# A ring of four places for the first raw weights, sums of four rows on VectorE for the second batch, and an earlier rank for it

## The chip, the cores and the metric

The kernel runs on one core of a Trainium2 chip. The metric is the time of one execution on the device in microseconds (us). A profile holds one execution; its time is the span of the trace and a little around it.

## What is computed

There are 8 batches, 8 heads, 576 positions and 64 columns in a head. The attention has two parts that are added: a global one on q, k and v averaged over groups of four rows, its result repeated four times, and a local one in which a row sees the rows less than four away. Heads side by side give x, 576 rows of 512 columns. Then x is mixed along the sequence and goes through a feed-forward network (FFN):

```python
q_d = q.reshape(B, H, S // 4, 4, D).mean(axis=3)          # k_d, v_d alike
x   = repeat(softmax(q_d k_d^T / 8) v_d, 4) + softmax(local q k^T / 8) v
u   = x + transpose(transpose(x) @ U @ V)                  # U 576 x 32, V 32 x 576
out = u + relu(u @ w_ch1) @ w_ch2                          # 512 -> 2048 -> 512
```

The weights, U and V come as 8-byte floats.

## The kernel before, in words

**Order of the work.** Every piece is an `op` with an engine, a duration, a rank (`prio`; lower goes first) and the buffers that it reads and writes. The class `Plan` is a list scheduler: it takes the ready op of the lowest rank on each engine, hands buffers out in the order in which they were asked for, and so writes a fixed order for each of the five engines TensorE (PE), VectorE (DVE), ScalarE (ACT), GpSimd (POOL) and SyncE (SP). All DMAs are issued from SP's one queue, which stands still where one of them has to wait.

**Batch 0.** Its four pairs of heads ("pair 0" to "pair 3") come first, each with `early_global` (scores `ps_s`, transposes `ps_t`, `ps_a`), `local_blocks` (`ps_b`, `ps_bt`, `ps_ba`) and `early_mix` (`ps_c`, `ps_x` into xT; `ps_hu`, which is x times U; then `ps_u`, which is added to xT on DVE at L743). From xT come uH on ACT and uL on POOL (L748).

**Weights.** There are 32 chunks of 511.8 KB, W1_0 to W1_15 and W2_0 to W2_15, read in the order W1_0 to W1_3, W1_4, W2_0, W1_5, W2_1 and so on up to W1_15 and W2_11 to W2_15. `load_w` asks for a raw buffer `wr`, issues its copy (L419), and `convert` makes the two halves of the chunk: ACT writes `half` (L347), DVE writes `y` (L350) and `c` (L352), ACT writes the high half W (L358), POOL the low half (L362). The raw buffer lies in the place in which the chunk itself will lie. `half` is one buffer, so conversions run in the order of the chunks. A copy waits until the conversion four chunks back has its `c`.

**FFN.** The tiles of columns are 4 of 288 (batches 0 and 1) and 9 of 384. A tile has 16 steps. `ffn1` of a step is 12 matmuls into `ps_h` (L959); ACT makes hH from it (L967), DVE hL (L968); `ffn2` is 12 matmuls into `acc` (L984), three steps later or more. Up to the nineteenth step, all but the second `ffn1` write the same PSUM bank, so that an `ffn1` waits for the hL before it.

**Batches 1 to 7.** Their attention lies between the FFN's steps: `late_global` (loads gq, gT and vr; sums of four rows; scores L790 and L783 in `ps_b`; `ps_t` L555; `ps_a` L569; stores up_s), `local_attn` (windows vl and ul, products Pt on POOL at L852, sums on DVE at L857, store x_s), `mix_part` (xL and Y from x_s; `ps_hu` L931; stk L936; `ps_u` L739). The sums of four rows are two POOL additions each: gh (L440) and smq or smk (L442) for q and k, and two (L530, L532) for each half of v. The buffers of these batches can be used only after the last op of batch 0's attention (`open_late`). `LEAD` is taken off the rank of batch 1's `late_global`. The first tile of batch 1 is tile 2: its FFN needs u of all four pairs.

## Time and profile before

| what | value |
|---|---|
| median of three runs | 1005.71 us (1005.45 to 1009.53) |
| the profiled execution | 1006.59 us |
| its span | 1004.8 us |
| PE busy in the span | 973.8 us, 97% |
| POOL, DVE, ACT busy | 571.8, 437.9, 345.4 us |
| mean granted clock of PE | 0.989 |

PE is busy nearly throughout, so that a time is read by where PE stood still or ran at half its clock, and by what it waited for there. The FFN begins at 66.46 us; the weights are all converted by about 122 us; tile 2 begins at 197.84 us.

### The profile page before, as it was taken

Reading aid. Unit: us, or ns where it says so; the run is one execution under the profiler, and the core shown is the slowest. Engines: PE = TensorE matmul, PEld = TensorE weight load, DVE = VectorE, ACT = ScalarE, POOL = GpSimd, SP = SyncE. Lnnn points to the kernel's source line nnn. Section 1 sums busy time; section 2 is a strip of 40 time slices with the busy share of each in tenths; the row PEclk is TensorE's granted clock in tenths of the full one; section 3 lists DMA queues with packets and bytes.
Section 4 is the critical chain, followed back from the end, with each engine's and each line's share of the span. In section 5 each row is a group of like instructions: output and inputs, shape, how many; then the busy total and the mean of one; then the engine's idle time right before and its main releaser. Section 6 shows DMA issues by size and latency. Waiting matters only on the chain.

```text
span 1004.8 us, 24588 instructions
## 1 busy us (share of the span) xinstructions
PE 973.8 (97%) x9896; PEld 940.5 (94%) x9896; DVE 437.9 (44%) x814; ACT 345.4 (34%) x1012; POOL 571.8 (57%) x640
## 2 busy tenths in 40 slices
PE   6879999899999999999999999999999999999998
PEld 4659999899999999999999999999999999999998
DVE  5686656535554444454434524354254222211211
ACT  4677544433343333243333233333332222111110
POOL 6586988957968657866665856665756112300100
PEclk9899999999999999999999999999999999999999
DMA  8949767647667546665454456465542021000000
GB/s 265 323 136 268 188 164 169 137 110 165 155 140 156 136 104 146 153 128 147 112 142 102 116 112 136 84 158 129 124 112 58 20 60 24 32 1 1 32 1 32
DMA packets 220906, 120.04 MB, mean 119 GB/s; under 512 B 174052, under 2 KB 196920, under 8 KB 220792
## 3 DMA queue, kind: packets, MB, share of 16 engines
q1 hardware_dynamic: 220792, 118.47, 48.0%
q8 instruction: 78, 1.28, 0.6%
q14 instruction: 36, 0.29, 0.1%
HBM read 87.57 MB, written 30.86 MB: 118 GB/s over the span
## 4 chain that ended last, share of the span: by engine, by line
PE 84%; DMA 4%; DVE 2%; SPq 1%; POOL 1%; issue 1%; ACT 0%; DVEq 0%; ACTq 0%
PE acc L984 37%; PE ps_h L959 37%; PE ps_a L569 2%; PE ps_b L790 2%; PE ps_t L555 2%; DMA wr<-in_W 2%; PE ps_hu L931 2%; PE ps_b L783 2%; DMA gq<-in_qT 1%; PE ps_u L739 1%; DVE acc L857 1%; DMA ul<-up_s 1%; DMA vr<-in_v 0%; POOL Pt L852 0%; SPq L806 0%
## 5 line engine op out<-in xcount | busy, mean ns | idle before, releaser
L984 PE MATMUL acc<-hH,W 128*128 128x384 f32 (+1 forms) x1664 | 443.1, 327 | 0.0
L959 PE MATMUL ps_h<-uH,W 128*128 128x384 f32 (+1 forms) x1376 | 358.1, 322 | 2.2 <-DVE hL L968 2.2
L984 PEld LDWEIGHTS acc<-hH,W 128*128 128x128 f32 x1664 | 297.6, 188 | 2.6
L984 PE MATMUL acc<-hL,W 128*128 128x384 f32 (+1 forms) x832 | 268.4, 323 | 0.0
L852 POOL TENSOR_TENSOR Pt<-vl,ms 128x896 f32<-128x896 f32 (+1 forms) x140 | 239.0, 1786 | 42.3 <-DMA vl<-in_vp 30.3
L968 DVE SCALAR_TENSOR_TENSOR hL<-ps_h,hH 128x384 fp32r<-128x384 f32 (+1 forms) x208 | 109.0, 524 | 331.0 <-ACT hH L967 330.5
L959 PEld LDWEIGHTS ps_h<-uH,W 128*128 128x128 f32 x1376 | 245.1, 189 | 3.5 <-DVE hL L968 2.6
L967 ACT ACTIVATE hH<-ps_h 128x384 fp32r<-128x384 f32 (+1 forms) x208 | 97.3, 468 | 370.2 <-PE ps_h L959 362.0
L959 PE MATMUL ps_h<-uL,W 128*128 128x384 f32 (+1 forms) x688 | 220.8, 321 | 1.6 <-POOL uL L748 1.6
L857 DVE TENSOR_REDUCE acc<-Pt 128x128 f32<-128x1024 f32 (+1 forms) x140 | 152.7, 1108 | 63.3 <-POOL Pt L852 29.7
L984 PEld LDWEIGHTS acc<-hL,W 128*128 128x128 f32 x832 | 156.8, 188 | 0.0
L959 PEld LDWEIGHTS ps_h<-uL,W 128*128 128x128 f32 x688 | 130.0, 189 | 1.8 <-POOL uL L748 1.8
L959 PE MATMUL ps_h<-u,W 128*128 128x384 f32 x432 | 98.1, 334 | 0.0
L846 ACT ACTIVATE Pt<-ul 128x128 f32<-128x128 f32 (+1 forms) x140 | 55.2, 436 | 91.3 <-DVE acc L857 62.3
L748 POOL TENSOR_TENSOR uL<-xT,uH 128x384 fp32r<-128x384 f32 (+2 forms) x52 | 40.9, 808 | 70.2 <-ACT uH L746 70.2
L923 POOL TENSOR_TENSOR xL<-xL,xH 116x640 fp32r<-116x640 f32 x28 | 43.8, 1566 | 61.9 <-ACT xH L922 50.7
L994 POOL TENSOR_TENSOR o<-uH,uL 128x384 f32<-128x384 f32 (+1 forms) x43 | 38.9, 936 | 70.0 <-DMA out_t<-o 70.0
L959 PEld LDWEIGHTS ps_h<-u,W 128*128 128x128 f32 x432 | 77.0, 188 | 0.0
L530 POOL TENSOR_TENSOR vr<-vr 72x256 f32<-72x256 f32 x56 | 41.1, 734 | 43.2 <-DMA vr<-in_v 41.5
L362 POOL TENSOR_TENSOR W<-c,W 128x512 fp32r<-128x512 f32 x32 | 40.8, 1283 | 18.1 <-ACT W L358 18.1
L743 DVE TENSOR_TENSOR xT<-ps_u,xT 128x384 f32<-128x384 f32 (+2 forms) x64 | 27.3, 451 | 28.1 <-PE ps_u L739 27.7
L790 PE MATMUL ps_b<-smk,smq 64*32 64x144 f32 x672 | 38.4, 292 | 0.0
(133 smaller groups left out, 893.3 us busy)
## 6 DMA issues: line engine op xcount, KB each, us to landing
wr<-in_W SPq DMA_DIRECT2D x32, 511.8 KB
vl<-in_vp SPq DMA_DIRECT2D x56, 240.0 KB
vr<-in_v SPq DMA_DIRECT2D x64, 144.0 KB
gT<-in_kT SPq DMA_DIRECT2D x28, 291.0 KB
gq<-in_qT SPq DMA_DIRECT2D x28, 288.0 KB
up_s<-od SPq DMA_DIRECT2D x168, 48.0 KB
ul<-up_s SPq DMA_DIRECT2D x28, 288.0 KB
x_s<-acc SPq DMA_DIRECT2D x28, 288.0 KB
```

The costliest lines, as they stand in the source:

```text
L362: pool_tt(1.0 * n, lambda: nc.gpsimd.tensor_tensor(out=lo_out(), in0=ta()[l0:], in1=hi_out()[l0:].bitcast(F32), op=ALU.subtract), [t, *own ...
L530: pool_tt(256, lambda x=x: nc.gpsimd.tensor_tensor(out=x()[:, :, 0:2, :], in0=x()[:, :, 0:2, :], in1=x()[:, :, 2:4, :], op=ALU.add), [x], ...
L748: pool_tt(n, lambda uH=uH, uL=uL, uf=uf, us=us: nc.gpsimd.tensor_tensor(out=uL.ap(hp, us), in0=uf(), in1=uH.ap(hp, us).bitcast(F32), op=AL ...
L790: nc.tensor.matmul(pg()[m:m + QL, a * SD:(a + 1) * SD], sq()[o, n:n + QL], sk()[o], start=True, stop=True)
L846: act(n * D, lambda n=n, ps=ps, Pt=Pt: nc.scalar.activation(Pt()[:, :n, :, 7], ul()[:, ps, :], AF.Copy), [ul], [(Pt, 1)], prio, 0.16)
L852: nc.gpsimd.tensor_tensor(out=Pt()[:, :n, :, 0:7].rearrange("p s d o -> p o s d"), in0=win, in1=at()[:, ps, :].rearrange("p s o -> p o s") ...
L857: dve(8.5 * n * D, lambda n=n, ps=ps, Pt=Pt: nc.vector.tensor_reduce(out=acc()[:, ps, :], in_=Pt()[:, :n], axis=AX.X, op=ALU.add), [(Pt, 0 ...
L923: pool_tt(640, lambda: nc.gpsimd.tensor_tensor(out=xL(), in0=xL().bitcast(F32), in1=xH().bitcast(F32), op=ALU.subtract), [xL, xH], [xL], prio)
L959: nc.tensor.matmul(ps()[:, :tn], W1[fc]()[:, w, dc, :], u.ap(dc), start=(n == 0), stop=(n == 3 * NDC - 1))
L967: last_h[i] = act(tn, lambda: nc.scalar.activation(hH()[:, :tn], ps()[:, :tn], AF.Relu), [ps], [hH], FIRST, 0.05)
L968: dve(tn, lambda: nc.vector.scalar_tensor_tensor(hL()[:, :tn], ps()[:, :tn], 0.0, hH()[:, :tn].bitcast(F32), op0=ALU.max, op1=ALU.subtract ...
L984: nc.tensor.matmul(ac[e]()[:, :tn], W2[fc]()[:, w, es], hx()[:, :tn], start=(fc == 0 and n == 0), stop=(fc == NFC - 1 and n == 2))
```

## The change

The first sixteen chunks no longer have their raw bytes in their own places: these go round a ring of four, the places of W2_11, W2_10, W1_15 and W1_14. (The first of them holds the table `pool` until `ps_p` has read it, the second pair 0's `vr`.) `LEAD` goes from 10.5 to 13. And in batch 1 the sums of four rows of q, k and v are single reductions on DVE instead of two POOL additions each. Nothing else is edited; the scheduler deals the order anew.

```diff
+    RAWS, NRAW = (f"W2_{NFC - 5}", f"W2_{NFC - 6}", f"W1_{NFC - 1}", f"W1_{NFC - 2}"), 16
     HOLD = 1.5
-    LEAD = 10.5
+    LEAD = 13
...
     def load_w(w, src, hi, lo, a, prio, dprio):
+        n = len(weights)
         weights.append(w)
-        raw = buf(wts, [128, 2 * CN], I32, "wr", w.tag + ":raw")
+        raw = buf(wts, [128, 2 * CN], I32, "wr", (RAWS[n % len(RAWS)] if n < NRAW else w.tag) + ":raw")
...
+    def pool_late(raw, lo, out, prio):
+        dve(S, lambda: nc.vector.tensor_reduce(
+            out=out()[:, 0:SD], in_=raw()[:, lo:lo + S].rearrange("p (j r) -> p j r", r=4), axis=AX.X, op=ALU.add),
+            [raw], [out], prio)
...
-        pool_halves(qr, 0, sq, False, prio)
-        pool_halves(kr, (SPAD - S) // 2, sk, False, prio)
+        if b == NE // HP:
+            pool_late(qr, 0, sq, prio)
+            pool_late(kr, (SPAD - S) // 2, sk, prio)
+        else:
+            pool_halves(qr, 0, sq, False, prio)
+            pool_halves(kr, (SPAD - S) // 2, sk, False, prio)
...
+            if b == NE // HP:
+                dve(512, lambda x=x, vs=vs: nc.vector.tensor_reduce(
+                    out=vs(), in_=x().rearrange("p a r d -> p a d r"), axis=AX.X, op=ALU.add), [x], [vs], prio)
+                continue
```

Three places of the order that this gives follow. Fifteen new lines move the numbers of the lines behind them: L419 becomes L421, L587 L602, L739 L754, L959 L974, L968 L983, L984 L999.

**SP's queue, from the table `ident` on.** `wr` is the raw copy of a chunk, `qt` and `kd` are q and k of a pair of batch 0, `vw`, `vwp` and `vr` its v. Before:

```order
L326 DMA ident_sb<-in_ident 128x128
L419 DMA wr<-in_W 128x2047
L587 DMA qt<-in_qT 128x576
L587 DMA kd<-in_kT 128x582
L605 DMA vwp<-in_vw 48x640 x2
L605 DMA vwp<-in_vw 48x512 x2
L455 DMA vr<-in_v 72x2x256 x2
L375 DMA ubr<-in_Ub 128x639
L379 DMA pool<-in_pool 128x144
L406 DMA vraw<-in_V 128x1151 x2
L419 DMA wr<-in_W 128x2047
L587 DMA qt<-in_qT 128x576
```

With the change:

```order
L327 DMA ident_sb<-in_ident 128x128
L602 DMA qt<-in_qT 128x576
L602 DMA kd<-in_kT 128x582
L620 DMA vwp<-in_vw 48x640 x2
L620 DMA vwp<-in_vw 48x512 x2
L462 DMA vr<-in_v 72x2x256 x2
L376 DMA ubr<-in_Ub 128x639
L380 DMA pool<-in_pool 128x144
L407 DMA vraw<-in_V 128x1151 x2
L602 DMA qt<-in_qT 128x576
L602 DMA kd<-in_kT 128x582
L421 DMA wr<-in_W 128x2047
```

The raw copies have moved behind the inputs of pairs 1 and 2. In all, 18 raw copies stand ahead of the first `gq` before, 13 with the change; of the other 19, the last three (W2_13 to W2_15) stand behind the store x_s of batch 1's pair 0 now, where they stood ahead of it. On POOL, 15 W subtractions (L362) stand ahead of the last uL of batch 0 before, 10 with the change; on DVE, 10 pairs of y and c stand between pair 0's second xT add and pair 3's u, where there were 8. On PE, pair 1's `ps_hu` and pair 3's `ps_s` and `ps_t` now stand behind the `ps_u` that this second add of pair 0 waits for.

**DVE in the first tile of the FFN.** `hL` is a step's result; from one hL to the next, before (from the thirteenth to the fifteenth; two reductions and a `y` stand ahead of the thirteenth):

```order
L968 SCALAR_TENSOR_TENSOR hL<-ps_h,hH 128x288
L352 SCALAR_TENSOR_TENSOR c_2026<-wr,y_h 128x512
L825 TENSOR_REDUCE lmx<-sc 128x9
L350 TENSOR_SCALAR y_h<-half 128x512
L352 SCALAR_TENSOR_TENSOR c_2091<-wr,y_h 128x512
L968 SCALAR_TENSOR_TENSOR hL<-ps_h,hH 128x288
L831 TENSOR_REDUCE lsm<-ms 128x9
L968 SCALAR_TENSOR_TENSOR hL<-ps_h,hH 128x288
```

With the change, from the thirteenth to the fourteenth:

```order
L983 SCALAR_TENSOR_TENSOR hL<-ps_h,hH 128x288
L351 TENSOR_SCALAR y_h<-half 128x512
L542 TENSOR_REDUCE vs<-vr 72x128
L353 SCALAR_TENSOR_TENSOR c_2081<-wr,y_h 128x512
L564 RECIPROCAL ri<-rr 128x3
L840 TENSOR_REDUCE lmx<-sc 128x9
L448 TENSOR_REDUCE smq<-gq 128x144
L351 TENSOR_SCALAR y_h<-half 128x512
L846 TENSOR_REDUCE lsm<-ms 128x9
L353 SCALAR_TENSOR_TENSOR c_2117<-wr,y_h 128x512
L983 SCALAR_TENSOR_TENSOR hL<-ps_h,hH 128x288
```

Between the first hL and the nineteenth, 15 y and 15 c of weights stand before, 19 y and 20 c with the change; besides, there are now 13 reductions for the sums of four rows (6 of q or k, 7 of v), and U's conversion (cu and Ust).

**PE at the beginning of tile 2.** The names ahead of the arrow are what is written. Before:

```order
L984 MATMUL acc_2479<-hH,W_15_2134 128x288
L984 MATMUL acc_2479<-hL,W_15_2134 128x288
L984 MATMUL acc_2479<-hH,W_15_2134 128x288
L931 MATMUL ps_hu<-xH,Ust 64x128 x5
L931 MATMUL ps_hu<-xL,Ust 64x128 x5
L739 MATMUL ps_u<-Vst,stk 128x288 x2
L555 MATMUL ps_t<-ident_sb,E 72x128 x6
L959 MATMUL ps_h<-uH,W_0_273 128x288
```

With the change, 15 `acc` matmuls stand between that `ps_hu` and its `ps_u`, and 21 between this and tile 2's first `ps_h`:

```order
L999 MATMUL acc_2532<-hH,W_14_2309 128x288
L999 MATMUL acc_2532<-hL,W_14_2309 128x288
L999 MATMUL acc_2532<-hH,W_14_2309 128x288
L754 MATMUL ps_u<-Vst,stk 128x288 x2
L999 MATMUL acc_2541<-hH,W_14_2309 128x288
L999 MATMUL acc_2541<-hL,W_14_2309 128x288
L999 MATMUL acc_2541<-hH,W_14_2309 128x288
```

Pair 3's `ps_hu` and `ps_u` of batch 1 now have other work behind each.

## Rows read from the trace of the kernel before

**Rows 1.** Table of stretches. Each line: the stretch (us from the start), its length, then busy time and instructions of PE, PEld, DVE, ACT, POOL, then the granted clock of PE (1.00 is full), the busy share of the DMA engines, GB/s.

```profile
0.00:48.60 48.60, 35.40 (x844) 26.13 (x844) 26.28 (x63) 28.02 (x88) 28.63 (x44) 0.89 0.94 290
48.60:66.50 17.90, 13.52 (x197) 10.36 (x198) 15.79 (x33) 14.82 (x36) 14.09 (x15) 0.90 0.27 108
66.50:126.00 59.50, 55.68 (x702) 53.49 (x702) 40.22 (x73) 37.50 (x96) 50.37 (x62) 1.00 0.86 229
...
72.50:138.60 66.10, 64.45 (x795) 62.69 (x796) 43.57 (x80) 37.85 (x98) 56.89 (x66) 1.00 0.81 209
198.20:201.30 3.10, 3.10 (x14) 3.10 (x14) 1.38 (x4) 0.97 (x4) 3.10 (x6) 0.50 0.70 192
40.00:45.00 5.00, 2.48 (x37) 1.87 (x35) 1.38 (x2) 2.18 (x5) 0.37 (x1) 0.93 1.03 405
```

**Rows 2.** The waits of PE from 66 us to the end: the waiting line, what it waited for, us in total, times, the longest.

```profile
PE ps_a L569 <- POOL vs L532: 2.2, 1, 2.2
PE ps_h L959 <- DVE hL L968: 2.2, 2, 1.1
PE ps_h L959 <- POOL uL L748: 1.6, 1, 1.6
PE ps_u L739 <- DVE stk L936: 1.5, 1, 1.5
```

**Rows 3.** PE in order of time, in the front: start, us, engine, line, what, count, and in brackets the idle time ahead of it with what ended it.

```profile
5.64 1.07 PE L622 MATMUL ps_b<-kd,qt 64*32 64x38 f32 x72 [1.93 <-DMA kd<-in_kT]
...
23.30 0.92 PE L622 MATMUL ps_b<-kd,qt 64*32 64x38 f32 x72 [1.41 <-DMA kd<-in_kT]
...
42.62 0.35 PE L723 MATMUL ps_hu<-od_e,Upl 112*32 112x64 f32 x3 [2.52 <-issue]
...
43.92 1.39 PE L475 MATMUL ps_s<-smk,smq_e 64*32 64x144 f32 x24
...
47.09 1.11 PE L493 MATMUL ps_t<-ident_sb,E_e 128*72 128x128 f32 x6
```

**Rows 4.** A stretch as in rows 1, but of the instructions on ps_hu alone (L720 and L723 of pair 1): PE, PEld, DVE, ACT.

```profile
38.90:44.00 5.10, 2.43 (x22) 1.76 (x22) 0.00 (x0) 0.00 (x0) 1.00 1.02 400
```

**Rows 5.** DVE in order of time: the second xT add of pair 0.

```profile
48.61 0.46 DVE L743 TENSOR_TENSOR xT<-ps_u,xT 128x288 f32<-128x288 f32 x1
```

**Rows 6.** The queue of SP in order of time: start, us that the issues took, line, what is moved, count.

```profile
33.74 11.56 SPq L419 DMA_DIRECT2D wr<-in_W  x13
66.69 0.33 SPq L587 DMA_DIRECT2D gq<-in_qT  x1
...
100.55 3.79 SPq L419 DMA_DIRECT2D wr<-in_W  x3
...
116.22 0.42 SPq L859 DMA_DIRECT2D x_s<-acc  x1
```

**Rows 7.** Groups of DVE instructions from 66 to 200 us, by form: line, operation, out<-in, shapes, count, busy us, mean ns of one, idle time ahead and what ended it.

```profile
L857 DVE TENSOR_REDUCE acc<-Pt 128x128 f32<-128x1024 f32 x20 | 24.3, 1215 | 7.2 <-POOL Pt L852 5.6 <-POOL vr L530 1.5
L968 DVE SCALAR_TENSOR_TENSOR hL<-ps_h,hH 128x288 fp32r<-128x288 f32 x32 | 14.5, 453 | 20.3 <-ACT hH L967 20.2
L352 DVE SCALAR_TENSOR_TENSOR c<-wr,y_h 128x512 int32<-128x512 int32 x18 | 12.3, 685 | 1.0
L350 DVE TENSOR_SCALAR y_h<-half 128x512 int32<-128x512 int16 x17 | 11.7, 691 | 5.4 <-ACT half L347 5.1
L857 DVE TENSOR_REDUCE acc<-Pt 128x64 f32<-128x512 f32 x5 | 3.4, 676 | 0.0
```

**Rows 8.** Instructions that write hL from 66 to 140 us: count, ns (least, median, most), start of the first and of the last.

```profile
L968 DVE SCALAR_TENSOR_TENSOR hL<-ps_h,hH x19: 444/451/458, 72.5 to 138.6; 128x288 fp32r<-128x288 f32 x19
```

**Rows 9.** Groups of POOL instructions from 66 to 200 us, by form, columns as in rows 7.

```profile
L362 POOL TENSOR_TENSOR W<-c,W 128x512 fp32r<-128x512 f32 x19 | 24.4, 1292 | 10.2 <-ACT W L358 10.2
L530 POOL TENSOR_TENSOR vr<-vr 72x256 f32<-72x256 f32 x12 | 8.8, 736 | 3.7 <-DMA vr<-in_v 2.0 <-PE ps_b L783 1.7
L532 POOL TENSOR_TENSOR vs<-vr 72x128 f32<-72x128 f32 x12 | 5.5, 460 | 0.3
L440 POOL TENSOR_TENSOR gh<-gq 128x288 f32<-128x288 f32 x7 | 4.8, 684 | 0.0
L442 POOL TENSOR_TENSOR smq<-gh 128x144 f32<-128x144 f32 x7 | 3.0, 432 | 0.1
```

**Rows 10.** Pieces of the chain that ended last, in order of time: start, us, what.

```profile
78.02 5.58 DMA gq<-in_qT
...
101.29 9.34 DMA wr<-in_W
...
119.24 1.58 PE acc L984 x12
120.82 1.60 PE ps_h L959 x12
```

**Rows 11.** POOL, then PE, in order of time: W subtractions of the last chunks, and the first matmul with W2_13.

```profile
114.22 2.55 POOL L362 TENSOR_TENSOR W<-c,W 128x512 fp32r<-128x512 f32 x2
...
123.68 0.40 PE L984 MATMUL acc<-hH,W 128*128 128x288 f32 x1
```

**Rows 12.** PE in order of time at the boundary of tile 2.

```profile
195.53 0.53 PE L739 MATMUL ps_u<-Vst,stk 128*128 128x288 f32 x2 [1.46 <-DVE stk L936]
197.21 0.98 PE L555 MATMUL ps_t<-ident_sb,E 128*72 128x128 f32 x6 [1.15 <-DVE xT L743]
```

## The prediction

> **What bounds the kernel now.** I read the table of stretches first. PE works in almost all of 1004.8 us, so the change can move only what PE stands idle or runs slowly. Up to pair 0's second xT add at 48.61 [rows 5] PE is busy 35.4 of 48.6 us, 13.2 idle; from there to the FFN 13.5 of 17.9, 4.4 idle, with DVE at 15.8, or 88% [rows 1]. The FFN's first stretch, 66.5 to 126, has 3.8 idle. The waits of PE say what the rest hangs on: in the FFN's beginning uL 1.6 and hL 2.2; at tile 2's boundary the stk of L936, 1.5; late in the run vs, 2.2 [rows 2]. At that boundary the reader is to see two idle times, 1.46 and 1.15 [rows 12], and then 3.1 us at a granted clock of 0.50, the lower of PE's two levels (1.2 GHz) [rows 1].
>
> All sums are made against the profiled execution, 1006.59 us, which lies 0.9 above the median of 1005.71.
>
> **A. The front: -4.5.** Behind pair 0's second xT add go pair 1's `ps_hu`, 2.43 [rows 4], pair 3's `ps_s`, 1.39, and its `ps_t`, 1.11 [rows 3]. PE's work up to there falls from 35.4 to 30.5. Of the 13.2 idle, about 5 is the start, up to the first scores at 5.64 [rows 3]; if that alone stays, the add comes at 35.5; if all stays, at 43.7. Two pieces can go since they stand beside raw copies that are now issued later: 1.41 of waiting for pair 2's `kd`, which a `wr` stood ahead of, and the hole of 2.52 ahead of L723, put down to "issue" [rows 3]. The hole lies in a stretch in which the DMA engines are busy at 1.03 and move 405 GB/s [rows 1], that is, in the 13 copies issued from 33.74 on [rows 6]. The Trainium skill (Runtime: NRT & Kernel Launch, Instruction fetch mechanics) says that an engine's sequencer fetches its next block of instructions through a DMA queue of its own, mostly hidden; by that rule such a hole hangs on the copies under way, and with fewer of them all 2.52 would go (the sum would be 1.3 lower), while by the row alone it may stay. I count it half, since most of the 13 copies ahead of gq still come about there: 13.2 - 1.4 - 1.3 = 10.5 idle, and the add at 41.0, 7.6 earlier.
>
> The stretch behind grows by what was moved. PE gets 13.5 + 4.9 = 18.4, DVE two more conversions of 0.691 + 0.685 [rows 7], so 15.8 + 2.75 = 18.5; at the 88% that DVE reached it lasts 21.0 instead of 17.9. The FFN begins at 62.0 instead of 66.5. Bounds: 35.5 + 21.0 = 56.5 (-10) and 43.7 + 21.0 = 64.7 (-1.8).
>
> **B. Scores one step earlier: +1.** The first late scores stand behind two steps of the FFN instead of three. gq was issued 0.2 after the FFN's beginning [rows 6] and a gq took 5.58 to land [rows 10]; gT is issued 0.4 later. With the sum (0.74, see C) the scores can begin 7.0 after the beginning; PE's two `ffn1` of 1.60 [rows 10] cover 3.2 of that. The stall of 3.8 takes the place of 1.6 for uL and 1.1 for hL. Bounds: 0, and +5 if gq lands in the 9.34 that a raw copy took.
>
> **C. DVE in the FFN's first steps: +4.** This is the term that speaks against the change. From the first hL to the nineteenth, 72.5 to 138.6 [rows 8], DVE was busy 43.6 of 66.1 us and PE 64.5 [rows 1]. The order adds four y and five c (6.2 by rows 7), U's conversion (about 2) and 13 sums. A sum of 576 is worked out from the two reductions of rows 7, 512 in 0.676 and 1024 in 1.215: 0.74; one of 72 x 512 is 0.68; together 9.2. Some attention is moved in as well (one more maximum, two `ps_u` adds, less one o). DVE comes to about 62, PE by the order to about 66. It would still fit, were it not for the single bank of `ps_h`: an `ffn1` cannot begin until the hL before it, so that what DVE has too much in one step is not made good in the next. From the tenth hL to the fifteenth DVE has by the order six y, seven c, five hL (9.0 + 2.3), four reductions of 1.215 and one of 0.676, three sums (2.2) and 1.7 of small ones: 20.7 us by these durations, 19.3 at the ratio of busy time to summed durations that the same count gives before (43.6 to 46.7), and PE there five `ffn1` (8.0), four `acc` groups of 1.58 [rows 10] and a `ps_t`: 14.8. That is 4.5 idle, of which the eased order before had next to nothing behind its second hL [rows 2]. I take 4. Bounds: 0, if the steps ahead lend their slack, and 8, if DVE also waits for raw copies and `half`, which stood for 5.1 in those rows. The Trainium skill (VectorE: DVE Perf Modes, Rules for kernel authors) advises against `tensor_reduce` on a hot path, since it runs at one element a cycle only; at the page's 0.96 GHz a sum of 576 would be 0.60, an estimate, and the term about 1 lower. The reductions of rows 7 have a fixed part besides, so I stay with theirs.
>
> **D. Tile 2's boundary: -4.2.** With 15 `acc` matmuls (2.0 us) between `ps_hu` and `ps_u` and 21 (2.8 us) ahead of tile 2's first `ps_h`, the idle 1.46 and 1.15 are covered, and with them goes the half clock behind them, which cost 3.1 x 0.5 = 1.55. The order can hold on the chip since POOL, busy throughout there, is relieved: a pair's sums cost it 2 x (0.68 + 0.43) + 2 x (0.74 + 0.46) = 4.6 [rows 9], four pairs 18, less five subtractions of 1.29 that come later, 6.5: 12 us net. Bounds: 0 and -4.2.
>
> **E. The rest: 0.** The order of batches 2 to 7 is dealt anew. Stalls like the 2.2 for vs [rows 2] may vanish or come; I take 0, with -4 and +4.
>
> Sum: -4.5 + 1 + 4 - 4.2 = -3.7, or 1002.9 for a profiled execution and **1002.0** for the median.
>
> **The rivals.**
>
> *DVE keeps up (faster).* If DVE's long steps are carried by the slack ahead of them, C is 0: 998.0. For it: 62 of 66 us is still below one, and DVE waited 20 us for hH [rows 7]. Against: the coupling by one bank.
>
> *One of the gains doesn't come (same).* The ring holds the front back: W1_0 may be copied only when `ps_p` has read its table, and a copy waits for the c four back; then the add stays at 43.7 and with the stretch's 21.0 A is -1.8, 1004.7. Or the boundary hangs on the DMAs of x_s, xL and Y instead of POOL; then D is 0, 1006.2.
>
> *The last raw copies come late (slower).* W2_13 to W2_15 stand behind x_s of pair 0 in the one queue. Before, they were issued at 100.55, and x_s at 116.22 [rows 6]; W2_13 was first used at 123.68 [rows 11]. With the change x_s would come at 111.7 if it only follows the FFN, but five raw copies more lie in the FFN's stretch: at its 229 GB/s for a share of 0.86 [rows 1], so 266 at full, 5 x 511.8 KB are 9.6 us, and x_s comes at 121.3. Then W2_13 lands 9.34 later [rows 10] and is subtracted 4.9 after that (110.65 to 115.5) [rows 10, 11]: with the issue 136.0. It is needed at 123.68 - 4.5 + 3.2 (two more `ffn1` ahead of it) + 5 (B and C) = 127.4. PE stands 8.6, and 1.6 of half clock follows: 1012.2. It costs from x_s at 112.7 on, and makes the kernel slower by over 0.5% from 119.8 on. Against: scores one step earlier and POOL's relief bring x_s forward.
>
> **How the numbers follow.** About 0.5%, 5 us, is what a measurement of this kernel can tell from no change; so faster ends at 1000.7, slower begins at 1010.7. My forecast has 0.44, its own range 998 to 1005.5 by the bounds of A and E; 0.17 of it lies below 1000.7. DVE keeping up has 0.20, a lost gain 0.16, late copies 0.20. Faster is 0.20 + 0.17 = 0.37, same 0.27 + 0.16 = 0.43, slower 0.20. The range goes from 993.5 (DVE keeps up and A is 4.5 better) to 1011, with a tenth left out at either end.
>
> **What would show it.** A: the first `ps_h` at 62, and no idle of 2.5 ahead of L738. B: scores behind the second `ffn1` with some 4 us idle for smq or smk. C: waits of `ps_h` for hL summing to 4 or more between the tenth and the nineteenth step, with DVE over 90% busy; if they sum to under 1.5, DVE keeps up. D: no idle at tile 2's boundary and a full clock behind it. The forecast is wrong if an `ffn1` or `acc` waits long for a W of the last three chunks, or if the FFN begins later than 65.

## The result: slower, and the profile after

The change makes the kernel slower: 1015.34 us median of four runs (1015.06 to 1016.14), beside 1006.49 for the kernel before on the same chip; the ratio over all these runs is 1.0084, with a 95% interval of 1.0060 to 1.0108. The forecast was 1002.0, with 1011 as the upper end. The profiled execution took 1016.14 us, its span 1014.4, which is 9.6 more than before. Runs of one and the same kernel lie up to some 0.5% to either side of their median (the kernel with the ring alone: 1009.3 to 1018.2), so single profiles are read for what waits, and all the runs of a kernel together for how much.

The table of stretches of the kernel after, columns as in [rows 1]; the first line ends at pair 0's second xT add, the fourth at the FFN's beginning, the fifth at tile 2's:

```profile
0.00:45.98 45.98, 31.91 (x795) 25.00 (x799) 16.30 (x47) 17.67 (x63) 21.02 (x38) 1.00 0.68 188
30.00:40.00 10.00, 7.98 (x111) 6.25 (x111) 1.78 (x4) 2.95 (x13) 4.83 (x7) 1.00 0.21 64
40.00:50.00 10.00, 9.97 (x260) 7.91 (x261) 6.22 (x16) 6.52 (x23) 1.59 (x2) 1.00 0.13 44
45.98:70.50 24.52, 18.96 (x249) 14.48 (x248) 19.51 (x39) 19.30 (x50) 15.49 (x15) 0.86 0.60 188
70.50:210.80 140.30, 129.09 (x1550) 122.95 (x1549) 96.99 (x176) 73.72 (x202) 100.33 (x99) 0.99 0.77 193
110.00:112.00 2.00, 2.00 (x24) 1.85 (x20) 2.00 (x5) 0.55 (x2) 0.00 (x0) 0.50 1.13 283
```

And of the kernel before, from the FFN's beginning to tile 2's:

```profile
66.46:197.84 131.38, 124.95 (x1550) 120.74 (x1549) 81.71 (x152) 68.31 (x190) 113.28 (x128) 1.00 0.76 189
```

Set against [rows 1], three stages answer. Up to the second xT add 45.98 us instead of 48.60; then 24.52 instead of 17.90 to the FFN, with DVE busy 19.5 of it; then 140.3 from the FFN's beginning to tile 2's, where the profile before has 131.4. Tile 2 so begins 13.0 later. What follows is 803.6 long, 807.0 before, and gives 3.4 back. The DMA engines are busy at 0.21 and 0.13 between 30 and 50 us; before, they were at 1.03 from 40 to 45 [rows 1].

PE in order of time in the front, columns as in [rows 3]: a new wait for pair 1's `kd`, a hole put down to "issue", and the FFN's first matmul.

```profile
12.45 0.81 PE L637 MATMUL ps_b<-kd,qt 64*32 64x38 f32 x54 [3.18 <-DMA kd<-in_kT]
...
32.02 0.47 PE L693 MATMUL ps_ba<-vwp,et 38*32 38x64 f32 x15 [4.66 <-issue]
...
70.52 0.29 PE L974 MATMUL ps_h<-uH,W 128*128 128x288 f32 x1
```

The hole that was 2.52 long and stood at 42.62 [rows 3] is 4.66 long now and stands at 32.02. DVE in order of time, columns as in [rows 5]:

```profile
45.98 0.46 DVE L758 TENSOR_TENSOR xT<-ps_u,xT 128x288 f32<-128x288 f32 x1 [1.01 <-PE ps_u L754]
...
48.59 0.68 DVE L353 SCALAR_TENSOR_TENSOR c<-wr,y_a 128x512 int32<-128x512 int32 x1
...
64.53 0.69 DVE L351 TENSOR_SCALAR y_a<-half 128x512 int32<-128x512 int16 x1 [1.45 <-ACT half L348]
...
108.59 1.05 DVE L542 TENSOR_REDUCE vs<-vr 72x128 f32<-72x512 f32 x1 [2.73 <-DMA vr<-in_v]
```

The first `c` of a weight is made at 48.59. In the profile before it was made at 12.47:

```profile
12.47 0.69 DVE L352 SCALAR_TENSOR_TENSOR c<-wr,y_a 128x512 int32<-128x512 int32 x1
```

So all the conversions of weights in the front, 10 up to the FFN where there were 15, fall behind the second xT add, and a `y` waits there for `half`. The last line of the list ahead of this one is a sum of v in the FFN: DVE stands 2.73 us, and all that is queued behind it with it, until a DMA brings `vr`. The queue of SP in order of time, columns as in [rows 6], then the matmuls of `ps_p` on PE, and then what SP waited for with the raw copies (us in total, times, the longest):

```profile
14.71 1.48 SPq L421 DMA_DIRECT2D wr<-in_W  x1
...
17.11 0.96 SPq L421 DMA_DIRECT2D wr<-in_W  x2
...
38.06 0.35 SPq L421 DMA_DIRECT2D wr<-in_W  x1
...
49.35 0.35 SPq L421 DMA_DIRECT2D wr<-in_W  x1
...
70.77 0.33 SPq L602 DMA_DIRECT2D gq<-in_qT  x1
...
124.08 0.65 SPq L874 DMA_DIRECT2D x_s<-acc  x1
...
130.44 1.71 SPq L421 DMA_DIRECT2D wr<-in_W  x1
```

```profile
36.53 1.49 PE L389 MATMUL ps_p<-Ublk,pool 128*64 128x32 f32 x24
```

```profile
SPq L421 <- DVE c L353: 25.8, 9, 10.4
...
SPq L421 <- PE ps_p L389: 7.5, 1, 7.5
```

The reader is to see the 7.5 us that one raw copy stands at the head of the queue for PE's `ps_p`. That is W1_0's, whose raw place holds the table. It is the fourth raw copy in the queue: three others went out by 18 us and lie there unconverted, since conversions run in the order of the chunks. It goes at 38.06, behind `ps_p` at 36.53. The later copies then wait for the `c` four back, 25.8 us in nine waits. In the FFN, x_s comes at 124.08 and the last raw copies at 130.44.

The waits of PE from 60 us on, columns as in [rows 2]:

```profile
PE ps_h L974 <- DVE hL L983: 4.3, 7, 1.4
PE ps_a L584 <- DVE vs L542: 3.2, 2, 2.3
PE ps_a L584 <- POOL vs L547: 1.9, 2, 1.4
PE ps_h L974 <- POOL uL L763: 1.6, 1, 1.6
```

PE in order of time in the FFN's first tile: the second and third step's work, a group of `ps_a`, and three `ffn1` that wait for an hL:

```profile
73.93 0.40 PE L974 MATMUL ps_h<-uL,W 128*128 128x288 f32 x1 [1.62 <-POOL uL L763]
...
76.57 0.40 PE L805 MATMUL ps_b<-smk,smq 64*32 64x144 f32 x5 [0.51 <-DVE smk L448]
...
109.70 0.58 PE L584 MATMUL ps_a<-vs,E 72*48 72x64 f32 x9 [2.26 <-DVE vs L542]
...
120.77 0.40 PE L974 MATMUL ps_h<-uH,W 128*128 128x288 f32 x1 [0.34 <-DVE hL L983]
...
129.50 0.40 PE L974 MATMUL ps_h<-uH,W 128*128 128x288 f32 x1 [1.36 <-DVE hL L983]
...
138.93 0.40 PE L974 MATMUL ps_h<-uH,W 128*128 128x288 f32 x1 [1.03 <-DVE hL L983]
```

And at tile 2's boundary, the places of [rows 12]:

```profile
205.46 0.46 PE L946 MATMUL ps_hu<-xL,Ust 116*64 116x128 f32 x5
...
207.79 0.43 PE L754 MATMUL ps_u<-Vst,stk 128*128 128x288 f32 x2
...
210.82 0.30 PE L974 MATMUL ps_h<-uH,W 128*128 128x288 f32 x1
```

At the boundary no bracket is left: `ps_hu`, `ps_u` and tile 2's first matmul run without idle time, as the moved order meant them to. In the first tile the waits for hL are seven instead of two, and there are new ones for sums of v.

### The profile page after: what moved, and what is told of

Same layout as the page of the kernel before. It is cut to its first block, busy times and chain, and to the rows that moved or that the text cites. A ratio compares the mean times of both kernels' runs of the same rounds, so it can differ in the third digit from the quotient of the medians.

```text
span 1014.4 us, 24558 instructions
## 1 busy us (share of the span) xinstructions
PE 977.5 (96%) x9896; PEld 942.5 (93%) x9896; DVE 446.3 (44%) x830; ACT 349.0 (34%) x1012; POOL 556.4 (55%) x608
## 4 chain that ended last, share of the span: by engine, by line
PE 75%; DMA 8%; POOL 3%; DVE 3%; SPq 2%; issue 1%; ACT 1%; DVEq 0%; ACTq 0%; POOLq 0%
PE acc L999 33%; PE ps_h L974 33%; DMA wr<-in_W 2%; PE ps_a L584 2%; PE ps_b L805 2%; POOL Pt L867 2%; PE ps_t L570 1%; PE ps_hu L946 1%; DMA vr<-in_v 1%; PE ps_b L798 1%; DMA vl<-in_vp 1%; DVE acc L872 1%; SPq L594 1%; DMA ul<-up_s 1%; DMA s_s<-se 1%
## 5 line engine op out<-in xcount | busy, mean ns | idle before, releaser
L999 PE MATMUL acc<-hH,W 128*128 128x384 f32 (+1 forms) x1664 | 442.4, 327 | 0.0
L974 PE MATMUL ps_h<-uH,W 128*128 128x384 f32 (+1 forms) x1376 | 357.7, 322 | 4.4 <-DVE hL L983 4.3
L999 PEld LDWEIGHTS acc<-hH,W 128*128 128x128 f32 x1664 | 297.5, 188 | 2.6 <-DVE o L1012 0.2
L999 PE MATMUL acc<-hL,W 128*128 128x384 f32 (+1 forms) x832 | 268.4, 323 | 0.0
L867 POOL TENSOR_TENSOR Pt<-vl,ms 128x896 f32<-128x896 f32 (+1 forms) x140 | 239.9, 1792 | 47.9 <-DMA vl<-in_vp 27.4
L983 DVE SCALAR_TENSOR_TENSOR hL<-ps_h,hH 128x384 fp32r<-128x384 f32 (+1 forms) x208 | 109.0, 524 | 325.6 <-ACT hH L982 324.4
L974 PEld LDWEIGHTS ps_h<-uH,W 128*128 128x128 f32 x1376 | 243.7, 188 | 7.5 <-DVE hL L983 6.2
L974 PE MATMUL ps_h<-uL,W 128*128 128x384 f32 (+1 forms) x688 | 220.1, 320 | 1.6 <-POOL uL L763 1.6
L999 PEld LDWEIGHTS acc<-hL,W 128*128 128x128 f32 x832 | 156.9, 189 | 0.0
L974 PEld LDWEIGHTS ps_h<-uL,W 128*128 128x128 f32 x688 | 129.2, 188 | 1.8 <-POOL uL L763 1.8
L974 PE MATMUL ps_h<-u,W 128*128 128x384 f32 x432 | 98.1, 334 | 0.0
L974 PEld LDWEIGHTS ps_h<-u,W 128*128 128x128 f32 x432 | 77.0, 188 | 0.0
L545 POOL TENSOR_TENSOR vr<-vr 72x256 f32<-72x256 f32 x48 | 35.4, 737 | 45.9 <-DMA vr<-in_v 45.9
```

Of the source, the lines that this page charges most:

```text
L867: nc.gpsimd.tensor_tensor(out=Pt()[:, :n, :, 0:7].rearrange("p s d o -> p o s d"), in0=win, in1=at()[:, ps, :].rearrange("p s o -> p o s") ...
L974: nc.tensor.matmul(ps()[:, :tn], W1[fc]()[:, w, dc, :], u.ap(dc), start=(n == 0), stop=(n == 3 * NDC - 1))
L983: dve(tn, lambda: nc.vector.scalar_tensor_tensor(hL()[:, :tn], ps()[:, :tn], 0.0, hH()[:, :tn].bitcast(F32), op0=ALU.max, op1=ALU.subtract ...
L999: nc.tensor.matmul(ac[e]()[:, :tn], W2[fc]()[:, w, es], hx()[:, :tn], start=(fc == 0 and n == 0), stop=(fc == NFC - 1 and n == 2))
```

## Experiments

In what follows, "first c" is the start of the first weight's `c` on DVE, "FFN" and "tile 2" the starts of these on PE, all in one profile; the ratio is to the kernel before on the same chip, over all runs of both.

| kernel | ring | sums on DVE | LEAD | first c | FFN | tile 2 | ratio (95%) |
|---|---|---|---|---|---|---|---|
| before | no | none | 10.5 | 12.47 | 66.46 | 197.84 | 1 |
| the change | yes | q, k, v | 13 | 48.59 | 70.52 | 210.82 | 1.0084 (1.0060 to 1.0108) |
| e1_ring_only | yes | none | 10.5 | 44.80 | 65.67 | 207.02 | 1.0088 (1.0061 to 1.0116) |
| e2_sums_only | no | q, k, v | 10.5 | 13.09 | 66.86 | 208.63 | 1.0105 (1.0075 to 1.0136) |
| e6_no_sums | yes | none | 13 | 47.88 | 68.76 | 207.76 | 1.0120 (1.0091 to 1.0150) |
| e7_other_first | yes, without the table's place | q, k, v | 13 | 12.39 | 68.72 | 203.26 | 1.0017 (0.9998 to 1.0036) |
| r1_change_again | yes | q, k, v | 13 | 49.43 | 71.73 | 209.27 | 1.0075 (1.0039 to 1.0110) |
| r2_first_only | W1_0 alone, in the table's place | q, k, v | 13 | 46.62 | 70.98 | 209.96 | 1.0082 (1.0056 to 1.0108) |
| r3_table_last | yes, the table's place fourth | q, k, v | 13 | 12.93 | 67.25 | 200.52 | 1.0053 (1.0031 to 1.0075) |
| r4_no_ring | no | q, k, v | 13 | 12.41 | 67.76 | 203.13 | 0.9998 (0.9971 to 1.0025) |
| s1_v_on_pool | yes | q, k | 13 | 48.33 | 70.64 | 211.78 | 1.0102 (1.0052 to 1.0151) |
| s2_no_ring_v_on_pool | no | q, k | 13 | 12.62 | 66.49 | 206.87 | 1.0131 (1.0072 to 1.0190) |
| y1_ring_short_y | yes | q, k, v | 13 | 46.24 | 65.25 | 200.68 | 1.0044 (1.0021 to 1.0067) |
| y2_no_ring_short_y | no | q, k, v | 13 | 12.30 | 65.85 | 199.24 | 0.9991 (0.9973 to 1.0009) |
| x_fill | yes | q, k, v | 13 | 48.87 | 70.72 | 207.86 | 1.0105 (1.0067 to 1.0143) |

Up to the FFN the traces show one and the same order on every engine in the change, e1_ring_only, e6_no_sums, r1_change_again, s1_v_on_pool and, but for its added matmuls, x_fill; and another one in the kernel before, e2_sums_only, e7_other_first, r4_no_ring and s2_no_ring_v_on_pool. With the first order the FFN begins at 65.67 to 71.73, 69.7 in the mean; with the second at 66.46 to 68.72, 67.3 in the mean. So the first order costs some 2.4 us there, and two single profiles can differ by more. Tile 2's beginning is not quite the same point everywhere: in e1, e2, e6, r2, s1 and s2, 24 or 25 matmuls more lie between the FFN's beginning and tile 2's (1574 or 1575, about 1550 in the others); in e2 the group ahead of tile 2 is 24 matmuls of `ps_a`, 2.05 us.

All diffs are against the changed kernel.

### Which part of the change

e1_ring_only takes the sums and the rank back, e6_no_sums the sums, e2_sums_only the ring and the rank:

```diff
-    LEAD = 13
+    LEAD = 10.5                 # e1, e2
...
-    RAWS, NRAW = (...), 16
+    RAWS, NRAW = (...), 0       # e2
...
-        if b == NE // HP:
+        if False:                # e1, e6: for q and k; the same for v
```

e7_other_first keeps the whole change, but puts W1_13's place into the ring where the table's stood:

```diff
-    RAWS, NRAW = (f"W2_{NFC - 5}", f"W2_{NFC - 6}", f"W1_{NFC - 1}", f"W1_{NFC - 2}"), 16
+    RAWS, NRAW = (f"W1_{NFC - 3}", f"W2_{NFC - 6}", f"W1_{NFC - 1}", f"W1_{NFC - 2}"), 16
```

Expected of e1_ring_only:

> The ring of four places alone: sums of four rows on POOL and LEAD as before. Theory 1 (the ring's first place is the cost: W1_0 may be copied only after ps_p has read the table pool, and the conversions, which go in order, are crowded ahead of the FFN and into its first tile): the first copy of W1_0 is issued at about 38 us, the first c comes at 47 to 49, the FFN begins at 69 to 71 as with the whole change, and the time is 1010 to 1014. Theory 2 (the sums on DVE are the cost): the FFN may begin late, but it has no waits of ps_a for vs on DVE and next to none for hL, and the time is within 3 us of before (1004 to 1009).

Expected of e2_sums_only:

> The sums of batch 1 on DVE alone: no ring, LEAD as before. Theory 1: the FFN begins at 66 to 67 as before; DVE has 16 conversions and 13 sums between the first hL and the nineteenth, so 2 to 4 us of waits for hL and vs, and against them the stall at tile 2's boundary is gone (-4): 1003 to 1008. Theory 2: the waits of the whole change (4.3 for hL, 3.2 for vs, and the half clock behind the 2.3 for vs) are all here, 6 to 8 us, and the time is 1010 to 1014.

Expected of e6_no_sums:

> The ring and LEAD, the sums on POOL as before. Theory 1: as the ring alone, 1010 to 1014, with the FFN at 69 to 71. Theory 2: within 3 us of before. If this differs from the ring alone by over 3 us, the rank (LEAD) matters, though alone it leaves every instruction in its place.

Expected of e7_other_first:

> The whole change, but with the place of W1_13 in the ring instead of that of W2_11, which holds the table pool: then no raw copy has to wait for ps_p. Theory 1: the order puts 18 raw copies ahead of the first gq as before, the first c comes before 20 us, the FFN begins at 66 to 67, and only the sums' cost is left, less the boundary's stall: 1003 to 1009. Theory 2: the ring's place does not matter, and the time is that of the whole change, 1013 to 1016. A third reading (any ring of four holds the copies back, since a place must be free of the chunk four back): the FFN begins later than 68 also here.

The ring alone costs 0.9%, as much as the whole change, and so it does with the rank (1.2%); the sums alone cost 1.05%, too. The parts do not add up; each edit deals batch 1's order anew. With the one place of the ring exchanged, everything else of the change kept, the kernel stands at 1.0017, with 1 within its interval. So it is not that raw bytes go round four places; it matters which place comes first.

Not all came as expected. The FFN of e1_ring_only begins at 65.67 and not at 69 to 71, earlier than before: its loss lies behind that. e2_sums_only is slower than theory 1 had it, and without theory 2's waits (1.4 for hL, 1.6 for vs). e6_no_sums, at 1017.16, is above its range and over 3 us above e1_ring_only's 1012.7, though the intervals overlap. The time of e7_other_first is theory 1's, but its FFN begins at 68.72, which was the mark of the third reading.

### The ring's first place

r1_change_again is the change unedited. The others grade the suspected wait: in r2_first_only W1_0 alone has its raw bytes in the table's place, in r3_table_last the table's place is the ring's fourth, r4_no_ring has no ring but the sums and the rank.

```diff
-    RAWS, NRAW = (f"W2_{NFC - 5}", f"W2_{NFC - 6}", f"W1_{NFC - 1}", f"W1_{NFC - 2}"), 16
+    RAWS, NRAW = (f"W2_{NFC - 5}", ...), 1                                                  # r2
+    RAWS, NRAW = (f"W1_{NFC - 1}", f"W1_{NFC - 2}", f"W2_{NFC - 6}", f"W2_{NFC - 5}"), 16   # r3
+    RAWS, NRAW = (f"W2_{NFC - 5}", ...), 0                                                  # r4
```

Expected of r1_change_again:

> The whole change once more, on the same chip and beside the same runs of before as the next three, for a second trace of it. Expected 1013 to 1017 (ratio to before 1.006 to 1.012), the hole of 4 to 5 us in pair 1's ps_ba with vwp again (if it belongs to the program and not to one execution), the FFN's beginning at 69 to 71 and tile 2 at 209 to 212.

Expected of r2_first_only:

> The whole change, but only W1_0 has its raw bytes in the place of the table pool; the fifteen others have their own places, so no copy waits for a place, only for the conversion four back. Theory 1a (the order of the conversions: all of them wait for W1_0, which waits for ps_p): nearly as slow as the whole change, 1010 to 1015, with 19 conversions left for the FFN's first 19 steps and the first c at 46 to 49. Theory 1b (the ring: a copy must wait until the place four back is free): nearly as fast as without a ring, 1003 to 1008.

Expected of r3_table_last:

> The whole change with the four places in another order: the one with the table pool is the fourth, so that W1_0 to W1_2 are converted early and W1_3 is the first that waits for ps_p. 17 conversions are left for the FFN's first 19 steps (20 with the whole change, 16 without the table's place). Theory 1: in between, 1005 to 1010, as the lag grows with the conversions that are left over. A rival (each new order of the attention of batch 1 has its own stalls, with no regard to the conversions): no such order; as slow as the whole change or faster than without a ring.

Expected of r4_no_ring:

> The sums on DVE and LEAD, with no ring. The order of the instructions is that of the ring with W1_13's place instead of the table's, so the two should agree within their spread: 1004 to 1008 (ratio 1.000 to 1.004). If this one is faster by over 3 us, the ring's waits cost something beyond the table; if it is as slow as the change, the place was not the cause.

DVE in order of time, the first `c` of a weight, in r2_first_only:

```profile
46.62 0.69 DVE L353 SCALAR_TENSOR_TENSOR c<-wr,y_a 128x512 int32<-128x512 int32 x1
```

and in r4_no_ring:

```profile
12.41 0.69 DVE L353 SCALAR_TENSOR_TENSOR c<-wr,y_a 128x512 int32<-128x512 int32 x1
```

One chunk in the table's place is enough: r2_first_only is as slow as the change. Conversions run in the order of the chunks through the one `half`, and W1_0's delay holds back all of them. With the table's place fourth, three conversions come early and about a third of the loss goes (0.53% left of 0.75 to 0.84, the intervals overlapping); with no raw bytes there, all goes. r4_no_ring has the same order of every engine's instructions as e7_other_first; the two differ in where the raw bytes lie and in the waits that this brings, and both stand at the time of before.

Of the change's order there are three traces (the change, r1_change_again, x_fill), of the other two (r4_no_ring, e7_other_first): in the mean the FFN begins at 71.0 and 68.2, tile 2 at 209.3 and 203.2. So most of the loss is there by tile 2, and less than half of that by the FFN. These kernels do not tell the wait from the order, however: with the place, the scheduler deals every engine's order anew, and e2_sums_only and s2_no_ring_v_on_pool lose as much with their first `c` at 13.09 and 12.62. That an order loses 1% by stalls of its own, the rival named for r3_table_last, is therefore not ruled out; y1_ring_short_y below keeps the order, and speaks against it for a part of the loss.

r4_no_ring is also the control for e2_sums_only, from which it differs in the rank alone: with the ring away, the rank is worth 1% to the sums (1.0105 to 0.9998). In e2_sums_only PE stands 2.9 for `stk` at tile 2's boundary, which r4_no_ring does not; it has 2.1 for an xT there.

### Sums of v back on POOL

Is it the sums of v that hold DVE's queue? s1_v_on_pool moves them back to POOL in the change, s2_no_ring_v_on_pool does so without the ring.

```diff
-            if b == NE // HP:
+            if False:                # s1, s2: for v
...
-    RAWS, NRAW = (...), 16
+    RAWS, NRAW = (...), 0            # s2
```

Expected of s1_v_on_pool:

> The whole change, but v's sums of batch 1 stay on POOL; those of q and k are on DVE. If a v sum that stands in DVE's queue ahead of its DMA is what costs in the FFN's first steps (waits of ps_a for vs on DVE, 3.2 us, and the half clock behind the longest), these go: 1009 to 1012. If the conversions left over are what costs, the waits for hL stay at 3 us or more and the time is within 3 us of the whole change (1012 to 1018).

Expected of s2_no_ring_v_on_pool:

> No ring, LEAD 13, the sums of q and k on DVE and those of v on POOL: the candidate for a version faster than both. Against the one without a ring and with all sums on DVE (equal to before) the waits of 2 us for vs behind its DMA should go; POOL gives back 2.4 of the 4.6 us per pair. Expected 1000 to 1006 beside a before of 1003 to 1006; if the order of batch 1 then stalls at tile 2's boundary, 1005 to 1009.

Neither is faster. In s1_v_on_pool the waits of `ps_a` for a sum of v on DVE are gone (3.2 us in the change's profile, but only 0.4 in that of r1_change_again), but the waits for hL stay (5.6 in six, 4.3 in seven with the change), and PE stands 2.8 for `stk`. In s2_no_ring_v_on_pool, PE in order of time, three waits in the stage that ends at tile 2:

```profile
179.47 0.51 PE L946 MATMUL ps_hu<-xL,Ust 116*64 116x128 f32 x5 [1.64 <-POOL xL L938]
...
202.95 0.82 PE L754 MATMUL ps_u<-Vst,stk 128*128 128x288 f32 x2 [3.60 <-DVE stk L951]
...
205.40 0.90 PE L584 MATMUL ps_a<-vs,E 72*64 72x64 f32 x12 [1.63 <-DVE xT L758]
```

s2_no_ring_v_on_pool was expected at 1000 to 1006 and took 1015.72. What is taken off DVE comes back as waits for POOL's xL and for a `stk` at the boundary. Without the ring, the sums of v on DVE are worth their price (0.9998 against 1.0131); with it the two intervals overlap. How much of the 1.3% of s2_no_ring_v_on_pool these waits are stays open.

### DVE's time taken away

If DVE's crowd before and in the FFN's first steps is what costs, then a conversion that costs DVE less should bring the time back with the ring and do little without it. In y1_ring_short_y and y2_no_ring_short_y `y` is computed for 16 of each 512 columns only and `c` repeats them; the kernel leaves out the rest of each `y`, so its weights are not the reference's. The order of all instructions is that of the change and of r4_no_ring.

```diff
+        ny = n if isinstance(wkey, str) else 16
...
-            out=yi(), in0=h().bitcast(I16)[:pp, :n], ...
+            out=yi()[:, :ny], in0=h().bitcast(I16)[:pp, :ny], ...
...
-            ti(), mid(), 13, yi(), ...
+            ti().rearrange("p (a b) -> p a b", b=ny), mid().rearrange(...), 13,
+            yi()[:, :ny].unsqueeze(1).broadcast_to([pp, n // ny, ny]), ...
```

Expected of y1_ring_short_y:

> The whole change, every instruction in its place on each engine, but the y of a weight's conversion computes 16 columns instead of 512, and c repeats them: the weights are not the reference's. So DVE loses 0.6 us for each of 32 chunks and nothing else changes. If the ring's cost is DVE, crowded by conversions ahead of the FFN and in its first steps: the FFN begins 3 to 6 us earlier (65 to 68), the waits for hL fall under 2, and the time falls by 5 to 9 us, to that of before or under it. If it is the hole of 4 to 6 us in PE's instructions and the late copies: the FFN begins at most 2 us earlier and the time falls by under 3 us.

Expected of y2_no_ring_short_y:

> The sums on DVE and LEAD without a ring, with the same short y, against which the other is read. If DVE is not the limit there, within 3 us of the same kernel with the whole y (1002 to 1008); if it falls by as much as the ring does (5 us or more), the short y helps whatever the order, and the ring's cost is not in DVE's crowding.

The stretch from the second xT add to the FFN, columns as in [rows 1], and PE's waits for hL, in y1_ring_short_y:

```profile
44.14:65.25 21.11, 17.06 (x249) 13.07 (x249) 14.48 (x39) 18.65 (x50) 15.47 (x16) 0.92 0.66 212
PE ps_h L977 <- DVE hL L986: 3.0, 6, 0.8
```

and in r1_change_again, with its waits for sums of v on DVE:

```profile
46.81:71.73 24.92, 20.07 (x250) 15.25 (x250) 19.54 (x39) 19.39 (x50) 15.49 (x16) 0.79 0.60 190
PE ps_h L974 <- DVE hL L983: 4.4, 8, 1.4
PE ps_a L584 <- DVE vs L542: 0.4, 2, 0.3
```

With 5.1 less busy time of DVE the stretch is 3.8 shorter, with as many matmuls on PE within one, and the waits for hL in the first tile fall from 4.4 to 3.0 us. Without the ring the same stretch falls, too, from 21.72 us in r4_no_ring to 18.42 in y2_no_ring_short_y. The FFN begins at 65.25 and tile 2 at 200.68, ten us ahead of the change. But of the 6.5 by which the FFN is ahead of r1_change_again's, 2.7 were there at the second xT add, ahead of which no weight is converted, so these are not the short `y`'s. In the time of all runs it is less, too: 1.0044 instead of 1.0075 to 1.0084, so 0.3 to 0.4% comes back with the ring, and 0.1% without it; by their intervals the two gains can't be told apart. The FFN's beginning met its mark; the waits for hL (under 2) and the time (5 to 9 us less) did not. So DVE's time sets the length of this stretch, and its crowding is likely to be a part of the loss, but the times do not show that; 0.4% remains whose place these runs don't show.

### The hole of "issue"

The hole was forecast to hang on the raw copies around it. In the change it grew where none is issued, between 18 and 38 us (the DMA engines are busy at 0.74 in it). Its place in PE's stream is steadier than its time: x_fill puts 60 small matmuls of zeros at the head of PE's queue and leaves all else as it is.

```diff
+    def fill():
+        for _ in range(60):
+            nc.tensor.matmul(pz()[:32, :32], wz[:, 0:32], wz[:, 0:32], start=True, stop=True)
+    op(PE, 0.0, fill, [], [pz], -20, lat=0.0)
```

Expected of x_fill:

> The whole change with 60 small matmuls of zeros added at PE's beginning, while it waits for the first inputs; every other instruction keeps its place on each engine. It tells what the hole of 4 to 6 us in pair 1's ps_ba (vwp), put down to issue, belongs to. If to the number of the instruction (PE out of instructions, since it got to that number too early): the hole moves to 60 matmuls earlier in the program, out of ps_ba and ahead of ps_t or ps_bt of that place, still behind some 474 matmuls of all. If to the program's place or to the time (what ps_ba reads, or the DMAs at 27 to 32 us): it stays in ps_ba. The time stays within 4 us of the whole change.

Stretches from the start to the hole, columns as in [rows 1]. In the change:

```profile
0.00:27.30 27.30, 17.89 (x474) 13.78 (x475) 11.55 (x34) 11.83 (x40) 16.19 (x31) 1.00 0.93 258
```

In x_fill, up to two moments inside its hole, and the group of matmuls that ends it, with what is left of its 80:

```profile
0.00:29.00 29.00, 22.56 (x602) 18.95 (x602) 12.07 (x35) 11.74 (x40) 16.16 (x31) 0.70 0.93 252
0.00:31.00 31.00, 22.56 (x602) 18.95 (x602) 12.07 (x35) 11.74 (x40) 16.16 (x31) 0.68 0.92 248
```

```profile
32.15 0.44 PE L702 MATMUL ps_ba<-vwp,et 38*32 38x64 f32 x7 [4.29 <-issue]
```

In r4_no_ring, and the hole there:

```profile
0.00:30.40 30.40, 20.37 (x473) 14.99 (x473) 15.83 (x41) 15.23 (x47) 18.07 (x33) 0.89 0.93 260
```

```profile
30.54 0.89 PE L693 MATMUL ps_ba<-vwp,et 38*32 38x64 f32 x68 [0.17 <-issue]
```

And in the kernel before, up to the beginning and just before the end of the hole of [rows 3]:

```profile
0.00:39.90 39.90, 29.25 (x727) 22.03 (x727) 21.72 (x53) 23.03 (x72) 26.90 (x43) 0.91 0.92 265
0.00:42.50 42.50, 29.45 (x727) 22.07 (x727) 23.11 (x55) 24.36 (x74) 27.37 (x43) 0.92 0.93 273
```

In x_fill nothing runs on PE between 29 and 31 us: 602 matmuls by either moment. The change has 474 ahead of its hole and r4_no_ring 473, though at another point of the program: 68 matmuls of its group are left there, 15 in the change. Behind the hole of x_fill 7 of the group's 80 are left, 15 in the change (32.02 above): it is 8 matmuls later in the program. The expectation, a shift by 60, missed; but the trace counts 128 more ahead of the hole, 8 of the program and 120 for the 60 that were put in: each of them has two records. In that count the hole keeps a raster: 474, 602, and 727 before, 128 and 125 apart. A smaller hole lies one step earlier, behind 347 matmuls in the change (0.62 long) and in r1_change_again (2.94), behind 475 in x_fill (1.21). A matmul has a weight load beside it, so some 255 instructions lie between. The hole is long where PE came to it early: 4.66 at 27.4, 4.29 at 27.9, but 1.50 at 30.3 in r3_table_last and 0.17 at 30.4 in r4_no_ring. The Trainium skill (Runtime: NRT & Kernel Launch, Instruction fetch mechanics) has an engine's instructions fetched in blocks of 256 by the sequencer's own DMA queue; the raster agrees with it. If the holes are that fetching, which no run here shows directly, then it is not hidden, as that section also has it, but cost 4.3 and 4.7 us in these rows. x_fill is no faster than the change (1.0105).

Such a hole alone doesn't explain the loss: e1_ring_only has one of 4.71 at the same matmul and is past it at 29.04, ahead of r4_no_ring (30.54), and loses 0.9%. But it stands ahead of `ps_p` in PE's order (32.02 and 36.53 in the change), so W1_0's copy waits for it, too; how much of the loss goes that way no run tells.

## Why the prediction was wrong

The forecast is off by 13.3 us: 8.6 in A and 8.0 in C, less 1.5 in B and 1.85 in E.

**The step that failed is A, the front.** It was put at -4.5 and came out at +4.1 (the FFN at 70.52 instead of 66.46). That it failed is safe: 62.0 was forecast, and no trace with this order of the front begins its FFN before 65.25. Its size is not: over the traces of the two orders it is some +2.4. The prediction knew that "W1_0 may be copied only when `ps_p` has read its table", and made it a rival that costs 2.7, the fallback to 43.7 and 21.0. It took the raw copies' new place in SP's queue for their time. But W1_0's copy, at its place in the queue, then stood 7.5 us, and the first `c` went from 12.47 to 48.59. Of A's 8.6, 5.0 lie in the first half: the second xT add came at 45.98 instead of 41.0, with 3.18 of waiting for `kd` that wasn't there before and a hole 2.1 longer, where 1.4 and 1.3 were to go. The other 3.5 lie in the second half, 24.5 instead of 21.0. DVE was busy 19.5 in it, where 18.5 was put; at 88% that is 22.2, and the other 2.3 it stood still, for `half` among others (1.6 in all, 64.53 above, where it was 0.4 before): it reached 80%. The mark that the prediction set itself, an FFN that begins after 65, was met. r2_first_only, e7_other_first and r4_no_ring show that W1_0's place, with the order that it brings, turns the loss on and off while the rest of the change stays. That it acts through DVE's time is made likely for a part of it by y1_ring_short_y; for the rest it is argued.

**B, +1**, came to -0.5: uL 1.62 and smk 0.51 (the first two rows of the FFN above) instead of 1.6 and 1.1. gq was issued right behind the FFN's beginning, as forecast, at 70.77.

**C, DVE in the FFN's first steps, was right in kind and too small by 8.0.** The forecast was 4, with waits for hL of "4 or more": they are 4.3 in all, 3.2 of them new. But the term as a whole is the 8.9 between FFN and tile 2, less B and D's 2.6 of idle: 8.9 + 0.5 + 2.6 = 12.0. To the hL waits come 3.2 for sums of v on DVE, of which 2.26 stands behind a reduction waiting 2.73 for its DMA (108.59 and 109.70 above), 1.4 for one on POOL, and about 1.7 of half clock around the stretch from 110 to 112. The prediction had counted DVE's work, and not that an input that is late holds DVE's whole queue. About 2.5 of the 12 isn't resolved: PE's busy time is 129.1 for 1550 matmuls, 125.0 for as many before. Not all of this repeats: in r1_change_again, the same kernel, the stage is 137.5 long instead of 140.3, with 4.4 for hL but 0.4 for the sums of v on DVE. By that trace C is some 9. Without the ring the stage is 134.5 and 135.4 long (e7_other_first, r4_no_ring), 3 to 4 more than before; what follows is as much shorter, so that the same sums cost nothing that can be measured in the whole.

**D, -4.2**, came as forecast: no idle at the boundary, and a full clock behind it (1.00 from 210.8 to 214.0).

**E, 0**, is -1.85: of the 3.4 that the rest is shorter, 1.55 is D's half clock.

A, B, C, D's idle part and the rest sum to 4.1 - 0.5 + 12.0 - 2.6 - 3.4 = 9.6, the difference of the spans.

**The rivals.** DVE keeping up is out. "A gain doesn't come" named the right cause, the table's place, with too small a price. The late raw copies gave the slower side its 0.20: x_s came at 124.08, beyond the 119.8 from which they were to decide, and the last copy at 130.44, but no `acc` and no `ffn1` waits for a W in the change. What had been late was the first copy, not the last.

**What stays open.** With the ring and short `y`, 0.4% of the loss remains; e2_sums_only and s2_no_ring_v_on_pool, with conversions in place, lose 1.0 and 1.3%, more than the waits at their boundary that are named here. From the FFN to tile 2 PE is busy 131.5 and 129.3 us in these two, at a granted clock of 0.96 and 0.97, where it was 125.0 at 1.00 before; the 24 or 25 more matmuls are some 2 of that. The rank by itself was not run, since by the scheduler it gives the same order of instructions as before. No version was faster than the kernel before; r4_no_ring and e7_other_first are equal to it.

## What to carry to other kernels

When a buffer gets another place, look up who holds that place and until when, and follow not the one transfer but the first link of every chain that runs in order behind it: here one copy out of 32 set when all conversions began. An instruction that waits for a DMA is priced by what stands behind it in its engine's queue, not by its own duration: one such wait of 2.73 on DVE held PE for 2.26. The beginning of the FFN in a single profile was good to some 3 to 4 us only; read such a stage from several. And when a scheduler deals the order anew, parts of a change don't add up; run each alone and all but one.

## What the hardware showed beyond that

- PE stood for 4.3 to 4.7 us with nothing that the profile shows to wait for, at places of its stream some 255 instructions apart, when it came there early, and for 0.17 when it came 2.5 to 3 us later (x_fill, the change, r4_no_ring above).
- A sum of 72 x 512 by strides, estimated at 0.68 from a reduction of 128 x 512, took 1.05 to 1.11 (the eight of the change, one at 108.59 above); one of 576 took 0.75 where 0.74 was estimated.
- The granted clock of a stretch is not always to be trusted: up to the second xT add it reads 1.00 in the change with PE busy 31.9 us for 795 matmuls, and 0.82 in r1_change_again, the same kernel, with 29.2 us for 795.
